# Summing rows on TensorE in loops instead of written-out matmuls

## The chip, the core and the metric

The kernel runs on one core of one Trainium2 chip. The metric is the device time of one execution in microseconds: 718.03 us before the change, the median of three runs (717.57 to 719.21).

## The reference

The input `x` has 384 x 384 pixels of 384 channels in bf16, `w1d` one number. The mean over all pixels gives a value per channel, a sigmoid makes a scale `s` of it, and every pixel is multiplied by that scale:

```python
g = jnp.einsum("bhwc->bc", x) / (H * W)
...
for i in range(k):                      # k is 1
    s = s + gp[:, i:i + C] * w1d[i]
s = _sigmoid(s)
return x * s[:, None, None, :]
```

So all of `x` has to be read before the first output can be written.

## The kernel before

The 147,456 pixels are laid out as 1152 rows. A row is 128 partitions x 384 channels, 96 KB. The whole input is 1152 rows; the buffer `arena` holds 275 of them. The kernel has two stages.

**Reading stage.** SP's queue loads all rows, one DMA for a stretch of rows, into places in `arena` (`load`, L235). TensorE sums them: for each row one matmul of an all-ones matrix (already loaded as weights) with the row's 128 x 384 values, all added up in one PSUM bank (`sum_rows`, L257, the matmul itself in `add_held`, L243, shown as L246 in the profile). 784 rows are *streamed*: summed and overwritten, to be loaded again later (`stream`, L354, "S" in `PLAN`). 368 rows are *kept*. 296 of these are packed: `take` (L364, "K") loads a group and has it summed, `fold` ("F") then packs four rows into the place of three, with bit operations on VectorE (L280 for one input, L286 for joins of two) and a test on ScalarE (L317). 72 rows stay raw; they are loaded last (L425), into areas named U, A, V, Y and T, followed by one last streamed row.

**Writing stage.** ScalarE makes the sigmoid (L433). VectorE and GpSimd unpack and scale the rows (L446), SP stores them (L473), and the streamed rows are loaded once more into places that come free. A planner in the kernel writes this order out; it does not depend on how the sums were made.

What sets the order: each engine runs its instructions in the order in which the kernel adds them to a recorder called `Flow` (L21 to L140). An entry names the rows that it reads and writes; `Flow.emit` turns that into semaphore waits. A DMA that loads into rows waits for the last matmul that summed what stood there, and for the last fold that used them. SP's queue is strictly in order, so a load that waits holds all loads behind it. A first join of a fold overwrites rows, so it waits until TensorE has summed these rows. With one entry a row (L263 to L269) every such wait is for the row concerned. An entry marked `block` has its wait issued by itself, ahead of whatever the entry issues.

`PLAN` (L398) is the order written by hand. An "S" entry has a place in `arena`, a number of rows and, in three entries, a third number: so many rows are summed at once, the rest (`due_rows`) only behind the next kept group, or ahead of the next stream. `keep_warm` (L271) adds 16 matmuls with an all-zero row (`s_bf`) in three places, so that TensorE is not idle for long.

Of the kernel before, what the change touches and what calls it, by code (L numbers as in the profile page):

```python
# [20 lines left out]
class Flow:  # L21
# [47 lines left out]
    def emit(self):  # L69
        nc = self.nc  # L70
        engines = {"SP": nc.sync, "ACT": nc.scalar, "PE": nc.tensor, "DVE": nc.vector, "POOL": nc.gpsimd}

        know = {e: {} for e in engines}

        def covers(k, d):
            return k.get(d.lane, 0) >= d.rank if d.dma else k.get(d.eng, -1) >= d.i

        for s in self.steps:
            k = know[s.eng]
            for d in sorted(s.deps, key=lambda d: -d.i):  # L80
                if covers(k, d):
                    continue
                s.waits.append(d)
                d.wanted = True
                for key, v in d.know.items():
                    if k.get(key, -1) < v:
                        k[key] = v
            s.know = dict(k)
            if s.dma:
                s.know[s.lane] = s.rank  # L90
            else:
                s.know[s.eng] = s.i

        count, sems = {}, {}
        for s in self.steps:
            if not s.dma and s.wanted:
                s.rank = count[s.eng] = count.get(s.eng, 0) + 1

        def sem(s):
            key = s.lane if s.dma else s.eng  # L100
            if key not in sems:
                name = f"f_{key[0]}{key[1]}" if s.dma else f"f_{key}"
                sems[key] = self.tc.alloc_semaphore(name)
            return sems[key]

        last = {}
        with self.tc.tile_critical(sync_engine=mybir.EngineType.Pool, no_gpsimd_drain=True):  # L107
            for s in self.steps:
                eng = engines[s.eng]
                waits = [(sem(d), d.rank * (16 if d.dma else 1)) for d in s.waits]  # L110
                hold = None if s.dma or not waits else waits.pop()
                for h, v in waits:
                    eng.wait_ge(h, v)  # L113
                if s.block and hold:
                    eng.wait_ge(*hold)
                    hold = None
                ins = s.emit()
                if ins is None:
                    continue
                if hold:  # L120
                    ins = ins._wait_ge(*hold)
                if s.dma:
                    ins.then_inc(sem(s), 16)
                    last[s.lane] = s
                elif s.wanted:
                    ins.then_inc(sem(s), 1)
            for lane, s in sorted(last.items(), key=lambda at: at[1].i):
                engines[lane[0]].wait_ge(sem(s), 16 * s.rank)
# [3 lines left out]
def kernel(  # L132
# [11 lines left out]
    nc = tc.nc  # L144
# [5 lines left out]
    RPP = HW // P  # L150
# [10 lines left out]
    U = 3 * PIECE + PAIRS * 3 * PAIR  # L161
    G0 = U + PAIR
    V = G0 + PAIRS * 3 * PAIR
    A = V + PAIR
    N_A = 39
    T = A + N_A
    Y = T + 2 * PIECE
# [19 lines left out]
    ones = pool.tile([P, P], bf16, name="ones")  # L187
# [4 lines left out]
    arena = pool.tile([P, ROWS, C], bf16, name="arena")  # L192
    s_bf = pool.tile([P, C], bf16, name="s_bf")
# [3 lines left out]
    bank0 = psum.tile([P, nc.PSUM_BANK_SIZE_BYTES // 4], f32, name="bank0")  # L197
# [11 lines left out]
    def rows(lo, n):  # L209
        return [("a", r) for r in range(lo, lo + n)]  # L210

    fl = Flow(nc, tc)
# [18 lines left out]


    summed = [0]

    def load(chunk, a, lo, hi):  # L235

        r0, n = chunk
        fl.add(
            "SP",
            lambda: nc.sync.dma_start(out=arena[:, a : a + hi - lo, :], in_=view(xf, r0, n)[:, lo:hi, :]),  # L240
            writes=rows(a, hi - lo), dma=True,
        )
    def add_held(rhs, stop=False):  # L243

        pe = nc.tensor
        return pe.add_instruction(  # L246
            mybir.InstMatmult(
                name=nc.get_next_instruction_name(),
                ins=[pe.lower_ap(rhs), pe.lower_ap(ones[:])],
                outs=[pe.lower_ap(acc)],  # L250
                start_tensor_calc=False, stop_tensor_calc=stop,
                tile_size=(P, P), tile_position=(0, 0), ldweights=False,
            )
        )


    def sum_rows(a, n):  # L257
        def emit(i, first, last):
            if first:
                return nc.tensor.matmul(acc, lhsT=ones[:], rhs=arena[:, i, :], start=first, stop=last)  # L260
            return add_held(arena[:, i, :], last)

        for i in range(a, a + n):  # L263
            first, last = summed[0] == 0, summed[0] == RPP - 1
            fl.add(
                "PE", lambda i=i, f=first, l=last: emit(i, f, l),
                reads=[("a", i), "ones"], writes=["bank0"],
            )
            summed[0] += 1  # L269

    def keep_warm(n):  # L271


        for _ in range(n):
            fl.add("PE", lambda: add_held(s_bf[:]), reads=["s_bf", "ones"], writes=["bank0"])

    def bits(dst, src, op0, s0, op1, s1, reads, writes):
        fl.add(
# [17 lines left out]
    def fold(k):  # L296
# [46 lines left out]
        reads=["ones", "w_bf"], writes=["bank0"],  # L343
# [4 lines left out]
        reads=["bank0"], writes=["w_sc"],  # L348
# [2 lines left out]
    streamed = [0]  # L351
    N_WARM = 16

    def stream(a, n, at_once=None):  # L354

        load(STREAMED, a, streamed[0], streamed[0] + n)
        if n > 40 and streamed[0] > N_STREAM // 2:
            keep_warm(N_WARM)
        m = n if at_once is None else at_once
        sum_rows(a, m)  # L360
        streamed[0] += n
        return a + m, n - m

    def take(g, lo=0, hi=None):  # L364

        a, q = GROUPS[g]
        hi = 4 * q if hi is None else hi
        load(KEPT, a + lo, c_group[g] + lo, c_group[g] + hi)
        sum_rows(a + lo, hi - lo)

    def of_group(g):
        return [i for i, piece in enumerate(pieces) if piece[0] == g]
# [20 lines left out]
    for i, (lo, hi, corner) in enumerate(corners):  # L393
# [2 lines left out]
    take(FIRST)  # L396
    fold(0)
    PLAN = [  # L398
# [6 lines left out]
    ]  # L405
    due_rows = (A, 0)
    for kind, a, *more in PLAN:
        if kind == "S":
            sum_rows(*due_rows)
            due_rows = stream(a, *more)  # L410
        elif kind == "K":
            take(a, *more)
            sum_rows(*due_rows)
            due_rows = (A, 0)
        else:
            for k in of_group(a):
                if not more or k == of_group(a)[more[0]]:
                    fold(k)
    assert streamed[0] == N_STREAM

    def take_raw(a, n):
        load(KEPT, a, raw(a), raw(a) + n)
        sum_rows(a, n)

    for a, n in [(U, 8), (A, 20), (A + 20, 11), (A + 31, 8), (V, 8), (Y + 1, 6), (T + 5, 4), (T + 2, 3), (T, 2)]:  # L425
        take_raw(a, n)
    load(STREAMED, LAST_ROW, N_STREAM, N_STREAM + 1)
    sum_rows(LAST_ROW, 1)
# [5 lines left out]
        reads=["bank0", "w_sc"], writes=["s_bf"],  # L434
# [291 lines left out]
    while True:  # L726
# [12 lines left out]
        if dve_at <= now:  # L739
# [4 lines left out]
            if landed and (ahead < PENDING or not can):  # L744
                chunk, a, lo, n, end = landed.popleft()
# [7 lines left out]
                if end or ahead < MERGE:  # L753
                    b, first = since
                    send(chunk, b, first, lo + n, stored(b, lo + n - first))
                    since = None
            elif can:
                f, t, then = turns.popleft()
# [5 lines left out]
        if alongside and alongside[0][0] <= now:  # L764
            _, chunk, a, lo, n = alongside.popleft()
            store(chunk, a, lo, lo + n)
            moves.append([now + LAT, n * ROW + PER_STORE, stored(a, n)])
        while waiting and waiting[0][0] <= now:
            _, n, then, chunk, a, lo, known = waiting.popleft()
# [14 lines left out]
        if bank_at is None and len(line) <= total - BANKS_AT and got and max(got)[0] > PS * 4 // 3:  # L784
            a = max(got)[1]
# [11 lines left out]
        if got and todo < N_STREAM:  # L797
            n, a = max(got)
            n = min(n, CAP, N_STREAM - todo)
# [62 lines left out]
```

## Time and profile before

| | before |
|---|---|
| median of 3 runs | 718.03 us (717.57 to 719.21) |
| span of the profiled execution | 715.5 us; no other time of this execution is given |
| moved by DMA | 303.68 MB, mean 424 GB/s |
| TensorE busy | 211.7 us, 1202 matmuls |
| VectorE busy | 467.4 us |
| ScalarE busy | 116.5 us |
| GpSimd busy | 98.1 us |
| TensorE waited for loads, in all | 46.9 us, 14 times |
| VectorE's joins waited for TensorE | 10.7 us, 6 times |

The page cuts the span into 40 slices of 17.9 us. The digits of an engine are tenths of busy time, those of PEclk tenths of full TensorE clock, and DMA is the mean busy share of the 16 DMA engines. In a timeline, a row has the start and the length of a run of equal instructions in us, the engine, the line and operation, the tiles, the shape and the count; the brackets have the idle time just ahead and what ended it. The chain of work lists what ended last, followed back from release to release. In a table of windows the columns are the window, its length, busy us and count of PE, PEld, DVE, ACT and POOL, then the granted TensorE clock, the DMA share and GB/s. A row of DMA issues ends with the size and the time from issue to landing.

### The profile page before, as it was taken

The page shows a single profiled execution, that of the slowest core. Times are in us where ns is not written, and L with a number is a line of the kernel's source. Part 1 is how long each engine was busy: PE and PEld are TensorE (multiplying, and loading weights), DVE is VectorE, ACT ScalarE, POOL GpSimd, SP SyncE. Part 2 cuts the span into 40 slices and gives each one's busy share as a digit, 9 for nine tenths or more (in the row PEclk, how much of TensorE's full clock was granted, in tenths as well). Part 3 has the DMA queues.
Part 4 walks back from the last instruction along what each step waited for, and adds up shares of the span by engine and source line. Part 5 has one row for each costly group of instructions (what it writes and reads, how often), then busy time and mean ns, then how long its engine had stood idle before and what let it go on. Part 6 is the DMA issues. An engine that isn't in the chain of part 4 may idle for free.

```text
span 715.5 us, 2029 instructions
## 1 busy us (share of the span) xinstructions
PE 211.7 (30%) x1202; PEld 0.3 (0%) x3; DVE 467.4 (65%) x383; ACT 116.5 (16%) x97; POOL 98.1 (14%) x46
## 2 busy tenths in 40 slices
PE   5667967999598680000000000000000000000000
PEld 0000000000000000000000000000000000000000
DVE  4600001799989849999999999999940597007840
ACT  3700001476667630000110000000000000000000
POOL 0000000000000005414233431167100000000000
PEclk9899998999899995555555555555555555555555
DMA  9999999999999989999999999999999999999997
GB/s 382 428 447 419 439 431 428 452 416 433 426 431 426 429 351 379 405 412 433 430 431 437 438 422 440 434 438 437 440 418 453 420 444 439 419 439 440 439 417 338
DMA packets 15996, 303.68 MB, mean 424 GB/s; under 512 B 1778, under 2 KB 2418, under 8 KB 5106
## 3 DMA queue, kind: packets, MB, share of 16 engines
q1 hardware_dynamic: 15984, 303.57, 99.1%
q8 instruction: 4, 0.07, 0.0%
q14 instruction: 6, 0.05, 0.0%
q10 hardware_dynamic: 2, 0.00, 0.0%
HBM read 190.32 MB, written 113.25 MB: 424 GB/s over the span
## 4 chain that ended last, share of the span: by engine, by line
DMA 48%; DVE 29%; PE 16%; ACT 1%; issue 1%; DVEq 0%; SPq 0%; another core or an unknown queue 0%; POOLq 0%
DMA arena<-in_x_dram 37%; DVE arena L446 20%; PE bank L246 16%; DMA out_dram<-arena 12%; DVE arena L280 5%; DVE arena L286 4%; ACT arena L317 1%; DVEq L107 0%; SPq L473 0%; SPq L240 0%; ACT s_bf L433 0%; SPq L113 0%; SPq L857 0%; POOLq L107 0%
## 5 line engine op out<-in xcount | busy, mean ns | idle before, releaser
L246 PE MATMUL bank<-arena,ones 128*128 128x384 bf16 x1151 | 203.6, 341 | 47.0 <-DMA arena<-in_x_dram 46.9
L280 DVE TENSOR_SCALAR arena<-arena 128x1536 uint16<-128x1536 uint16 (+2 forms) x199 | 140.4, 750 | 105.7 <-DMA arena<-in_x_dram 98.8
L446 POOL TENSOR_TENSOR arena<-arena,s_bf 128x768 bf16<-128x768 bf16 (+3 forms) x42 | 97.9, 2336 | 426.3 <-ACT bank L437 268.0
L446 DVE TENSOR_TENSOR arena<-arena,bank 128x3072 bf16<-128x3072 bf16 (+13 forms) x61 | 138.0, 2304 | 4.3 <-DMA arena<-in_x_dram 3.6
L446 DVE TENSOR_TENSOR arena<-arena,s_bf 128x5376 bf16<-128x5376 bf16 (+4 forms) x27 | 76.5, 2901 | 95.1 <-DMA arena<-in_x_dram 84.9
L286 DVE TENSOR_TENSOR arena<-arena 128x3072 uint16<-128x3072 uint16 (+2 forms) x90 | 117.6, 1307 | 13.5 <-PE bank L246 10.7
L317 ACT ACTIVATE arena<-arena 128x3072 uint16<-128x3072 uint16 (+1 forms) x38 | 102.4, 2696 | 146.0 <-DVE arena L280 146.0
L563 PE MATMUL bank<-odd,ones 128*128 128x1 bf16 x1 | 0.2, 185 | 259.4 <-DVE odd L558 259.4
L384 ACT COPY arena<-bank 128x512 uint32<-128x512 uint32 (+2 forms) x8 | 4.2, 533 | 87.3 <-DMA out_dram<-arena 87.2
L246 PE MATMUL bank<-s_bf,ones 128*128 128x384 bf16 x48 | 8.3, 326 | 0.0
L317 ACT ACTIVATION_READ_ACCUMULATOR arena<-arena 128x1 f32 x38 | 7.1, 186 | 0.0
L384 ACT COPY bank<-arena 128x512 uint32<-128x512 uint32 (+2 forms) x8 | 3.8, 528 | 0.0
L260 PE MATMUL bank<-arena,ones 128*128 128x384 bf16 x1 | 0.5, 477 | 6.8 <-DMA arena<-in_x_dram 6.8
L433 ACT ACTIVATE s_bf<-bank,w_sc 128x384 bf16<-128x384 f32 x1 | 0.6, 581 | 9.5 <-PE bank L246 9.5
L830 ACT ACT_TABLE_LOAD x1 | 1.3, 1283 | 0.7 <-PEq L846 0.7
L337 DVE MEMSET ones<- 128x128 bf16 x1 | 0.2, 165 | 1.1 <-PEq L846 1.1
L342 PE MATMUL bank<-w_bf,ones 1*128 1x1 bf16 x1 | 0.2, 182 | 2.1 <-DMA w_bf<-in_w1d_dram 2.1
L347 DVE TENSOR_SCALAR w_sc<-bank 128x1 f32<-128x1 f32 x1 | 0.2, 158 | 0.9 <-PE bank L342 0.9
L567 DVE CAST odd_i<-bank 128x1 int32<-128x1 f32 x1 | 0.2, 159 | 0.3 <-PE bank L563 0.3
L437 ACT COPY bank<-s_bf 128x192 uint32<-128x192 uint32 x1 | 0.3, 322 | 0.0
L563 PEld LDWEIGHTS bank<-odd,ones 128*128 128x128 bf16 x1 | 0.1, 103 | 517.7 <-DVE odd L558 517.7
L384 ACT COPY arena<-rest 128x64 uint32<-128x64 uint32 x1 | 0.2, 244 | 0.0
(10 smaller groups left out, 1.4 us busy)
## 6 DMA issues: line engine op xcount, KB each, us to landing
arena<-in_x_dram SPq DMA_DIRECT2D x3, 6912.0 KB, 36.2
out_dram<-arena SPq DMA_DIRECT2D x3, 6912.0 KB, 28.4
arena<-in_x_dram SPq DMA_DIRECT2D x4, 4608.0 KB, 24.5
arena<-in_x_dram SPq DMA_DIRECT2D x6, 3072.0 KB, 19.6
out_dram<-arena SPq DMA_DIRECT2D x6, 3072.0 KB, 21.6
arena<-in_x_dram SPq DMA_DIRECT2D x2, 6144.0 KB, 31.5
arena<-in_x_dram SPq DMA_DIRECT2D x2, 4992.0 KB, 23.1
arena<-in_x_dram SPq DMA_DIRECT2D x1, 8160.0 KB, 26.5
```

Of the source, the lines that this page charges most:

```text
L246: return pe.add_instruction(mybir.InstMatmult(name=nc.get_next_instruction_name(), ins=[pe.lower_ap(rhs), pe.lower_ap(ones[:])], outs=[pe. ...
L260: return nc.tensor.matmul(acc, lhsT=ones[:], rhs=arena[:, i, :], start=first, stop=last)
L280: lambda: nc.vector.tensor_scalar(out=dst, in0=src, scalar1=s0, scalar2=s1, op0=op0, op1=op1),
L286: "DVE", lambda: nc.vector.tensor_tensor(out=dst, in0=a, in1=b, op=op), reads=reads, writes=writes
L317: lambda: nc.scalar.activation(out=y, in_=y, func=ACTF.Copy, accum_out=seen[:, 2 * k + i : 2 * k + i + 1]),
L337: fl.add("DVE", lambda: nc.vector.memset(ones[:], 1.0), writes=["ones"])
L384: "ACT", lambda: nc.scalar.copy(dst.bitcast(u32), src.bitcast(u32)), reads=reads, writes=writes
L433: lambda: nc.scalar.activation(out=s_bf[:], in_=acc, func=ACTF.Sigmoid, scale=w_sc[:, 0:1]),
L437: "ACT", lambda: nc.scalar.copy(s_ps.bitcast(u32), s_bf[:].bitcast(u32)), reads=["s_bf"], writes=["bank0"]
L446: lambda: vec.tensor_tensor(out=v, in0=v, in1=s[:, None, :].to_broadcast([P, n, C]), op=Op.mult),
L563: lambda: nc.tensor.matmul(votes, lhsT=ones[:], rhs=odd[:], start=True, stop=True),
L830: nc.scalar.preload_act_table(ACTF.Sigmoid)
```

## The change

Three things change, all in the reading stage.

- **Loops.** `sum_rows` adds a stretch of 16 rows or more as one `block` entry that holds a hardware loop on TensorE, and the one to three rows left over as single matmuls. The number of matmuls a turn is picked from 4, 5 and 3 by the number of instructions that it leaves; here it is 3 for all 27 loops, which take 966 rows in 322 turns. The loop entry and the rows behind it read the whole stretch, so whoever waits for one row of it waits for the last matmul of the stretch. `keep_warm` becomes a loop of 4 matmuls a turn.
- **Nothing put off.** The third numbers in `PLAN` are gone: every stream is summed whole before the group behind it.
- **Sizes.** The stream of 80 rows has 84, the last one 15 in place of 19 and starts four rows higher; the loads of A are 24 and 7 rows in place of 20 and 11.

```diff
+    BODY, LOOPED = 4, 16
...
-        for i in range(a, a + n):
-            first, last = summed[0] == 0, summed[0] == RPP - 1
+        def looped(a, m, body):
+            with nc.Fori(a, a + m, body, engines=[mybir.EngineType.PE]) as i:
+                for j in range(body):
+                    add_held(arena[:, bass.ds(i + j, 1), :])
+            return None
+
+        if summed[0] == 0:
+            fl.add("PE", lambda i=a: emit(i, True, False), reads=[("a", a), "ones"], writes=["bank0"])
+            summed[0] += 1
+            a, n = a + 1, n - 1
+        m = 0
+        if n >= LOOPED:
+            body = min((4, 5, 3), key=lambda b: 2 * b + (n - 1) % b)
+            m = (n - 1) // body * body
+        if m:
             fl.add(
-                "PE", lambda i=i, f=first, l=last: emit(i, f, l),
-                reads=[("a", i), "ones"], writes=["bank0"],
+                "PE", lambda a=a, m=m, b=body: looped(a, m, b), reads=rows(a, m) + ["ones"], writes=["bank0"], block=True
+            )
+            summed[0] += m
+        for i in range(a + m, a + n):
+            last = summed[0] == RPP - 1
+            fl.add(
+                "PE", lambda i=i, l=last: emit(i, False, l),
+                reads=rows(a, n) if m else [("a", i), "ones"], writes=["bank0"],
             )
             summed[0] += 1
...
-        for _ in range(n):
-            fl.add("PE", lambda: add_held(s_bf[:]), reads=["s_bf", "ones"], writes=["bank0"])
+        def looped():
+            with nc.Fori(0, n, BODY, engines=[mybir.EngineType.PE]):
+                for _ in range(BODY):
+                    add_held(s_bf[:])
+            return None
+
+        fl.add("PE", looped, reads=["s_bf", "ones"], writes=["bank0"], block=True)
...
-        ("S", 156, 80), ("K", 1), ("F", 1), ("S", 68, 48), ("K", 2), ("F", 2), ("S", 172, 52), ("K", 3), ("F", 3),
-        ("S", 68, 48), ("K", 4), ("S", 220, 39, 16), ("K", 5), ("F", 4), ("F", 5), ("S", 92, 24, 19), ("S", 196, 24),
+        ("S", 156, 84), ("K", 1), ("F", 1), ("S", 68, 48), ("K", 2), ("F", 2), ("S", 172, 52), ("K", 3), ("F", 3),
+        ("S", 68, 48), ("K", 4), ("S", 220, 39), ("K", 5), ("F", 4), ("F", 5), ("S", 92, 24), ("S", 196, 24),
...
-    for a, n in [(U, 8), (A, 20), (A + 20, 11), (A + 31, 8), (V, 8), (Y + 1, 6), (T + 5, 4), (T + 2, 3), (T, 2)]:
+    for a, n in [(U, 8), (A, 24), (A + 24, 7), (A + 31, 8), (V, 8), (Y + 1, 6), (T + 5, 4), (T + 2, 3), (T, 2)]:
```

The order of TensorE's instructions at the end of the reading stage, before the change: the last stream of 19 rows (it waits for f_SP8, the semaphore of its load), the 8 rows of U (f_SP9), the first 20 rows of A (f_SP10) and its next 11 (f_SP11).

```order
L246 MATMUL bank_71<-arena,ones 128x384 [waits f_SP8]
L246 MATMUL bank_71<-arena,ones 128x384 x18
L246 MATMUL bank_71<-arena,ones 128x384 [waits f_SP9]
L246 MATMUL bank_71<-arena,ones 128x384 x7
L246 MATMUL bank_71<-arena,ones 128x384 [waits f_SP10]
L246 MATMUL bank_71<-arena,ones 128x384 x19
L246 MATMUL bank_71<-arena,ones 128x384 [waits f_SP11]
```

The same place after the change. The stream has 15 rows. The load into A has 24: the wait for it stands at the jump into a loop, whose body is three register programs (shown as ISA) and three matmuls with an add and a branch, run seven times; three matmuls follow.

```order
L247 MATMUL bank_71<-arena,ones 128x384 [waits f_SP8]
L247 MATMUL bank_71<-arena,ones 128x384 x14
L247 MATMUL bank_71<-arena,ones 128x384 [waits f_SP9]
L247 MATMUL bank_71<-arena,ones 128x384 x7
L265 UNCONDITIONAL_BRANCH [waits f_SP10]
L265 ISA
L247 MATMUL bank_71<-arena,ones 128x384
L247 ISA
L247 MATMUL bank_71<-arena,ones 128x384
L247 ISA
L247 MATMUL bank_71<-arena,ones 128x384
L265 REGISTER_ALU
```

What moved: four rows from ahead of that load to behind its wait, and the wait from a matmul to the loop's entry.

VectorE in one fold of a kept group of 32 rows, before: the three joins that overwrite summed rows wait for f_PE (TensorE) by themselves, one in the first half of the fold, one at its end and one in the next half.

```order
L286 TENSOR_TENSOR arena<-arena 128x3072 [waits f_DVE,f_PE]
L280 TENSOR_SCALAR arena<-arena 128x1536 [waits f_ACT]
L280 TENSOR_SCALAR arena<-arena 128x1536
L280 TENSOR_SCALAR arena<-arena 128x1536 [waits f_DVE]
L280 TENSOR_SCALAR arena<-arena 128x1536
L286 TENSOR_TENSOR arena<-arena 128x1536 [waits f_DVE,f_PE]
L286 TENSOR_TENSOR arena<-arena 128x1536 [waits f_DVE]
L280 TENSOR_SCALAR arena<-arena 128x3072 [waits f_ACT]
```

After: only the first join of the group waits for TensorE, and that wait is for the last matmul of the group.

```order
L310 TENSOR_TENSOR arena<-arena 128x3072 [waits f_DVE,f_PE]
L304 TENSOR_SCALAR arena<-arena 128x1536 [waits f_ACT]
L304 TENSOR_SCALAR arena<-arena 128x1536
L304 TENSOR_SCALAR arena<-arena 128x1536 [waits f_DVE]
L304 TENSOR_SCALAR arena<-arena 128x1536
L310 TENSOR_TENSOR arena<-arena 128x1536 [waits f_DVE] x2
L304 TENSOR_SCALAR arena<-arena 128x3072 [waits f_ACT]
```

What moved: the later joins' waits for TensorE are gone, and the first one has to wait for 32 rows.

More of the change, by code (lines that the diff above doesn't have):

```diff
@@ L352, with stream @@
     N_WARM = 16
-    def stream(a, n, at_once=None):
+    def stream(a, n):
         load(STREAMED, a, streamed[0], streamed[0] + n)
@@ L358, in stream @@
             keep_warm(N_WARM)
-        m = n if at_once is None else at_once
-        sum_rows(a, m)
+        sum_rows(a, n)
         streamed[0] += n
-        return a + m, n - m
     def take(g, lo=0, hi=None):
@@ L398 @@
     PLAN = [
[3 rows of a table removed]
[3 rows of a table added]
         ("K", 6), ("F", 6), ("S", 220, 20), ("K", 7, 24, 32), ("S", 240, 19), ("K", 7, 0, 12), ("F", 7, 0),
         ("S", 220, 20), ("K", 7, 12, 24), ("S", 240, 19), ("K", 8, 0, 12), ("S", 220, 20), ("K", 8, 24, 32),
[1 row of a table removed]
[1 row of a table added]
     ]
-    due_rows = (A, 0)
     for kind, a, *more in PLAN:
         if kind == "S":
-            sum_rows(*due_rows)
-            due_rows = stream(a, *more)
+            stream(a, *more)
         elif kind == "K":
             take(a, *more)
-            sum_rows(*due_rows)
-            due_rows = (A, 0)
         else:
```

4 rows, old and new, of the table PLAN are left out of this document.

## The prediction

> **What bounds the kernel now.** I read the page first, then the chain of work that ended last, then TensorE's timeline. In the page I look at the span, at what the engines did, and at the two strips "PE" and "DMA".
>
> ```profile
> span 715.5 us, 2029 instructions
> PE 211.7 (30%) x1202; PEld 0.3 (0%) x3; DVE 467.4 (65%) x383; ACT 116.5 (16%) x97; POOL 98.1 (14%) x46
> PE   5667967999598680000000000000000000000000
> DMA  9999999999999989999999999999999999999997
> HBM read 190.32 MB, written 113.25 MB: 424 GB/s over the span
> ```
>
> The DMA engines are busy from end to end; moving bytes is the bound. TensorE works only in the first 15 of 40 slices. The change moves no byte, so it can matter at one place: where the reading stage ends and everything waits for the sums. The chain there reads (start, length, what):
>
> ```profile
> 245.00 11.81 DMA arena<-in_x_dram
> 256.85 10.59 PE bank L246 x63
> 267.46 0.59 ACT s_bf L433
> 268.07 12.70 DVE arena L446 x11
> ```
>
> The last large load lands at 256.8, TensorE adds 63 rows without a break until 267.4, then come the sigmoid, the first scaling and the first store. All that follows starts from there, so a microsecond at 267.4 is a microsecond at the end. No time is given for the profiled execution apart from its span; 718.03, the median of the runs, lies 2.5 us above the span, and I add shifts to 718.03.
>
> TensorE's timeline gives its pace, and what stood ahead of each burst (idle us, then what ended it):
>
> ```profile
> 38.50 11.79 PE L246 MATMUL bank<-arena,ones 128*128 128x384 bf16 x62 [3.71 <-DMA arena<-in_x_dram]
> 53.45 10.89 PE L246 MATMUL bank<-arena,ones 128*128 128x384 bf16 x66 [3.16 <-DMA arena<-in_x_dram]
> 68.31 19.39 PE L246 MATMUL bank<-arena,ones 128*128 128x384 bf16 x108 [3.97 <-DMA arena<-in_x_dram]
> ...
> 167.36 13.16 PE L246 MATMUL bank<-arena,ones 128*128 128x384 bf16 x80 [0.33 <-DMA arena<-in_x_dram]
> 183.44 2.76 PE L246 MATMUL bank<-arena,ones 128*128 128x384 bf16 x16 [2.93 <-DMA arena<-in_x_dram]
> 190.71 34.19 PE L246 MATMUL bank<-arena,ones 128*128 128x384 bf16 x194 [4.50 <-DMA arena<-in_x_dram]
> 227.28 5.36 PE L246 MATMUL bank<-arena,ones 128*128 128x384 bf16 x32 [2.39 <-DMA arena<-in_x_dram]
> 234.28 5.20 PE L246 MATMUL bank<-arena,ones 128*128 128x384 bf16 x31 [1.64 <-DMA arena<-in_x_dram]
> 241.56 6.68 PE L246 MATMUL bank<-arena,ones 128*128 128x384 bf16 x40 [2.08 <-DMA arena<-in_x_dram]
> 250.44 4.55 PE L246 MATMUL bank<-arena,ones 128*128 128x384 bf16 x27 [2.20 <-DMA arena<-in_x_dram]
> 256.85 10.57 PE L246 MATMUL bank<-arena,ones 128*128 128x384 bf16 x63 [1.86 <-DMA arena<-in_x_dram]
> ```
>
> 80 matmuls in 13.16 us is 164.5 ns each, the pace at full clock. After 3.71 us of idling 62 took 11.79, not 10.20; after 3.97, 108 took 19.39, not 17.77: 1.6 us lost each time. After 3.16 nothing was lost (66 in 10.89). The 63 at the end come after 1.86 us and run at full pace.
>
> **The change part by part.**
>
> *Last loads (+0.9).* The first load into A grows from 20 to 24 rows. The rows behind it are 63 in both: 20+11+8+8+6+4+3+2+1 and 24+7+8+8+6+4+3+2+1. The stretch
>
> ```profile
> 112.00:172.00 60.00, 59.67 (x353) 0.00 (x0) 42.63 (x59) 32.29 (x23) 0.00 (x0) 0.96 1.00 431
> ```
>
> moves 431 GB/s, so a row (128 x 384 x 2 bytes = 98,304 B) takes 0.228 us, and four make the load land 0.9 us later, with as much work behind it. The four rows taken from the last stream went to the 84-row one, so the loads before stand where they stood.
>
> *Clock at the tail (+1.6).* TensorE now has 15+8 rows, not 19+8, ahead of that load: it finishes 4 x 0.168 = 0.7 us sooner (4.55/27 each) and waits 0.9 longer. Idle: 1.86+0.7+0.9 = 3.4 us, and 3.7 with the loop's entry (next). That is the 3.71 of the burst at 38.50, which lost 1.6 us. Bounds: 0 (the 3.16 row) and 1.6; I take 1.6, the nearest row. The granted clock (the third number from the end) shows how sharp this is:
>
> ```profile
> 184.00:188.40 4.40, 2.21 (x14) 0.00 (x0) 4.17 (x7) 3.31 (x3) 0.00 (x0) 1.00 1.02 441
> 188.50:191.80 3.30, 1.09 (x4) 0.00 (x0) 2.79 (x4) 1.93 (x3) 0.00 (x0) 0.50 1.04 447
> ```
>
> The burst at 183.44 ended at 186.2, and the clock had halved by 188.5, after 2.3 us of idling. [...]
>
> *Loops: pace (0) and entry (+0.3).* By the code 966 rows go through 27 loops, all with three matmuls a turn, 322 turns. A turn has 3 x 164.5 = 493 ns of matmul to hide three register programs, one add and one branch. The trace shows no register instruction on TensorE; the nearest rows are its own branch and semaphore step, beside SP's branch (min/median/max ns):
>
> ```profile
> L857 PEldq EVENT_SEMAPHORE  x2: 51/51/51, 714.8 to 715.5; - x2
> L857 SPq COMPARE_BRANCH  x1: 33/33/33, 0.7 to 0.7; - x1
> ...
> L857 PEldq COMPARE_BRANCH  x1: 168/168/168, 0.8 to 0.8; - x1
> ```
>
> With 51 for each register step, 4 x 51 + 168 = 372 ns, hidden, with 121 ns left to issue three matmuls. If each costs 168, 5 x 168 = 840 ns, 280 a row. I take hidden, being nearer the plain step; the other end is rival 2. Below zero is excluded: the matmuls themselves are unchanged. At an entry the wait stands ahead of a register move and a jump, so the first matmul follows a landing by 51+168 and a register program: 0.3 us. It counts once on the path, after the 24-row load; earlier entries fall into idle time or behind queued matmuls.
>
> *Kept rows: later folds (0).* A loop reads its load as one block, so VectorE's first join of a group waits for all 32 rows, where it waited for 8. VectorE's timeline:
>
> ```profile
> 128.71 1.76 DVE L286 TENSOR_TENSOR arena<-arena 128x3072 uint16<-128x3072 uint16 x1 [7.43 <-PE bank L246]
> ...
> 208.95 1.90 DVE L280 TENSOR_SCALAR arena<-arena 128x3072 uint16<-128x3072 uint16 x3 [2.17 <-DMA arena<-in_x_dram]
> 211.18 1.76 DVE L286 TENSOR_TENSOR arena<-arena 128x3072 uint16<-128x3072 uint16 x1 [0.33 <-PE bank L246]
> 240.37 0.96 DVE L280 TENSOR_SCALAR arena<-arena 128x3072 uint16<-128x3072 uint16 x1 [0.20 <-ACT arena L317]
> 243.37 1.03 DVE L280 TENSOR_SCALAR arena<-arena 128x1536 uint16<-128x1536 uint16 x2 [2.04 <-DMA arena<-in_x_dram]
> ```
>
> For the join at 128.71 TensorE had to do 80+8 matmuls; now 84+32: 28 x 0.1645 = 4.6, plus 0.9 for the larger load, 5.5 us. For the join at 211.18 it is 24 x 0.1645 = 3.9. After that only 0.20+2.04 us of VectorE's waiting can absorb it, so the last fold ends some 1.7 us later (up to 5.5 if little is absorbed). Behind it SP holds the load into V and all smaller ones. Those have cover (KB, us from issue to landing; V's, the kept group's at 97.7, and the very first, which met an empty queue):
>
> ```profile
> arena<-in_x_dram SPq DMA_DIRECT2D x1, 768.0 KB, 7.1
> ```
> ```profile
> arena<-in_x_dram SPq DMA_DIRECT2D x1, 3072.0 KB, 21.6
> ```
> ```profile
> arena<-in_x_dram SPq DMA_DIRECT2D x1, 2400.0 KB, 8.1
> ```
>
> An empty queue costs 8.1 - 25 x 0.228 = 2.4 us. V's 8 rows move in 1.8, so 7.1-1.8-2.4 = 2.9 us of delay is free: 1.7 costs nothing, 5.5 would land the last row 2.6 us later, near 269.5, still before TensorE ends. The load of the first kept group now waits for 64 rows of the stream that it overwrites, not 16: 48 x 0.1645 = 7.9 us, against 21.6-7.3-2.4 = 11.9 free.
>
> *Sums no longer put off (0).* The order changes only at group 5: 23 rows of the 39-row stream come ahead of its 32. They take 3.8 us and fall into the 4.50 us that TensorE idled before 190.71. SP's 27 extra jumps at 33 ns each come while it waits for loads to come free.
>
> Sum: 0.9 + 1.6 + 0.3 = +2.8: the sums end near 270.2, the kernel at 718.03 + 2.8 = **720.8**. As the loads end before that, TensorE alone sets it.
>
> **Rivals.** *1, the clock stays up:* +1.2, 719.2. For it: 3.4 us lies between 3.16 (kept) and 3.71 (lost). Against: the halving after 2.3 us.
>
> *2, the loop cannot be issued in 493 ns.* At 600 ns a turn, the 197 turns after 111.8 cost 21 us more, against 17.9 us that TensorE idles there (0.33+2.93+4.50+2.39+1.64+2.08+2.20+1.86): 722 to 739 as none or all of it shows, say 730. At 840 ns it is 68 us, or 768 to 786. It decides once a turn passes 493 ns. For it: TensorE's 168 ns branch is five times SP's. [...] The trace has TensorE's fetches as packets, four in the reading stage, one here between 50 and 60 us (packets, MB, share of 16 engines):
>
> ```profile
> q8 instruction: 1, 0.02, 0.6%
> ```
>
> [...]
>
> *3, faster: those packets stood in the loads' way.* If all four hit the same DMA engine, they delay its last load by 3.8 us; a program with 281 matmuls for 1202 needs about one, so loads land 2.9 us sooner. With the clock up: 718.03 - 2.9 + 1.2 = 716.3; with the 1.6 lost, 717.9, no change. It decides if the packets add up on one engine. Against: four in 213 us, and TensorE's own 10.6 us behind the load stays.
>
> **How the numbers follow.** 720.8: 0.35. Rival 1: 0.15. Rival 2: 0.22 around 730, 0.05 at 768 and more; 2b 0.05. Rival 3: 0.10 at 716.3, 0.08 at 717.9. A measurement can tell about 0.2%, 1.4 us, from no change. Slower: 0.35+0.22+0.05+0.05 = 0.67; same (719.2, 717.9): 0.15+0.08 = 0.23; faster: 0.10. The range 717.0 to 733.0 leaves out rival 3's fast end and the upper part of rival 2, about 0.2; 720.8 alone would have 719 to 722.
>
> **What would show it.** Right: TensorE's last burst of 63 begins near 258, after over 3 us of idling, with a granted clock of 0.50 at its start, and ends near 270. Rival 2: bursts of loops over 170 ns a row, VectorE's joins late by tens of us. Rival 3: fewer instruction packets and the last loads landing before 266. I am wrong if the sums end at 267.5 or sooner.

## The result and the profile after

The changed kernel takes 739.38 us (median of four runs, 739.23 to 740.54); the kernel before, run beside it on the same chip, 718.15 us (717.57 to 719.21). The ratio is 1.0291, 95% interval 1.0272 to 1.031: 21.2 us slower. The forecast was 720.8, its range ended at 733.0. The profiled execution of after took 740.54 us, with a span of 738.2; its span is 22.7 us longer than that of before.

The page of after, the lines that answer to those of before, and the strip of DMA rates:

```profile
span 738.2 us, 3668 instructions
PE 243.7 (33%) x1202; PEld 0.3 (0%) x3; DVE 467.2 (63%) x383; ACT 116.5 (16%) x97; POOL 98.1 (13%) x46
PE   4689988999899877000000000000000000000000
DMA  9999999989597996999999999999999999999997
GB/s 392 434 431 431 454 400 423 441 341 409 231 419 325 414 424 238 404 421 421 430 436 443 428 438 425 433 445 421 438 441 435 434 422 439 432 426 441 443 431 316
```

The number of matmuls is the same (1202), but they keep TensorE busy for 243.7 us instead of 211.7, and 16 slices instead of 15 have TensorE in them. The DMA strip, all 9s in the reading stage before but for an 8 at its end, now has 8, 5, 7 and 6 in it, with 231 to 341 GB/s in the four worst slices: loads came late. From slice 17 on the DMA engines are as busy as before.

The end of the reading stage in the chain of waits of after:

```profile
265.34 10.92 DMA arena<-in_x_dram
276.26 0.23 issue
276.49 13.32 PE bank L247 x63
289.81 0.02 issue
289.83 0.59 ACT s_bf L451
290.42 0.02 issue
290.45 12.70 DVE arena L464 x11
```

The pieces are the same as before, but the sums end at 289.81, not at 267.44: 22.4 us of the 22.7. The last burst itself grew only from 10.59 to 13.32; the other 20 us are that it starts at 276.49 and not at 256.85. So the cause lies ahead of the tail. TensorE's timeline of after:

```profile
53.88 54.69 PE L247 MATMUL bank<-arena,ones 128*128 x238 [0.33 <-DMA arena<-in_x_dram]
111.91 26.87 PE L247 MATMUL bank<-arena,ones 128*128 x116 [3.34 <-DMA arena<-in_x_dram]
138.62 2.76 PE L247 MATMUL bank<-s_bf,ones 128*128 128x384 bf16 x16
...
183.92 0.65 PE L247 MATMUL bank<-arena,ones 128*128 x3 [0.27 <-issue]
184.84 0.65 PE L247 MATMUL bank<-arena,ones 128*128 x3 [0.27 <-issue]
...
200.76 44.65 PE L247 MATMUL bank<-arena,ones 128*128 x215 [0.16 <-issue]
246.32 6.54 PE L247 MATMUL bank<-arena,ones 128*128 x32 [0.91 <-DMA arena<-in_x_dram]
253.45 6.37 PE L247 MATMUL bank<-arena,ones 128*128 x31 [0.59 <-DMA arena<-in_x_dram]
260.73 7.84 PE L247 MATMUL bank<-arena,ones 128*128 x40 [0.90 <-DMA arena<-in_x_dram]
269.03 3.90 PE L247 MATMUL bank<-arena,ones 128*128 128x384 bf16 x23 [0.47 <-DMA arena<-in_x_dram]
276.49 13.31 PE L247 MATMUL bank<-arena,ones 128*128 x63 [3.56 <-DMA arena<-in_x_dram]
```

Before, TensorE worked in bursts and idled for a load ahead of nearly each. Now 238 rows run in one piece, at 54.69/238 = 230 ns a row where full clock gives 164.5, and between 111.91 and 245 it waits for no load at all. It is no longer ahead of the loads; it paces them. The chain of waits from 111.9 to 289.8, by line, says the same: TensorE makes up 77.6% of it, and loads are on it only from 239.10 on (before, from 111.8 to 267.4, TensorE has 60.3% and loads 32.2%):

```profile
by line: PE bank L247 77.6%; DMA arena<-in_x_dram 15.4%; issue 7.1%
```

What fills the time are the loops' own instructions on TensorE's sequencer (the part of the engine that issues its instructions, PEldq in the rows), all at the loop's line (duration min/median/max in ns, then first and last start), and the register programs in front of the other matmuls of a turn:

```profile
L265 PEldq FUSED_REGOPS  x322: 59/59/59, 9.4 to 280.7; - x161
L265 PEldq ALU_OP  x322: 36/36/42, 9.8 to 281.1; - x161
L265 PEldq COMPARE_BRANCH  x322: 76/208/341, 9.9 to 281.2; - x161
```
```profile
L247 PEldq FUSED_REGOPS  x644: 55/55/55, 9.6 to 280.9; - x161
```

322 turns, as counted. The five steps of a turn take 59 + 2 x 55 + 36 + 208 = 413 ns. The turn takes longer than they do. One loop seen alone (the adds between 95 and 107 us):

```profile
L265 PEldq ALU_OP  x17: 36/36/36, 95.0 to 106.5; - x17
```

Sixteen turns in 11.5 us are 0.72 us a turn, 240 ns a row. The loads bring a row every 228 ns.

VectorE and SP show what hangs on that. The joins that overwrite summed rows waited 39.9 us for TensorE, seven times, where it was 10.7 us and six times before (the last figure of the row):

```profile
L310 DVE TENSOR_TENSOR arena<-arena 128x3072 uint16<-128x3072 uint16 (+2 forms) x90 | 117.7, 1307 | 42.1 <-PE bank L247 39.9
```

SP issues its last nine loads, from the 24 rows for A on, between 265.34 and 282.3 (the row has the start of the first and the time to the end of the last); before, the last one goes out at 260.2:

```profile
265.34 16.98 SPq L241 DMA_DIRECT2D arena<-in_x_dram  x9
```

### The profile page after: what moved, and what is told of

Read it like the earlier page. It is cut to its first block, busy times and chain, and to the rows that moved or that the text cites. A ratio compares the mean times of both kernels' runs of the same rounds, so it can differ in the third digit from the quotient of the medians.

```text
span 738.2 us, 3668 instructions
## 1 busy us (share of the span) xinstructions
PE 243.7 (33%) x1202; PEld 0.3 (0%) x3; DVE 467.2 (63%) x383; ACT 116.5 (16%) x97; POOL 98.1 (13%) x46
## 4 chain that ended last, share of the span: by engine, by line
DMA 40%; DVE 28%; PE 24%; issue 3%; SPq 0%; DVEq 0%; another core or an unknown queue 0%; ACT 0%; POOLq 0%
DMA arena<-in_x_dram 29%; PE bank L247 24%; DVE arena L464 20%; DMA out_dram<-arena 11%; DVE arena L304 5%; DVE arena L310 3%; DVEq L107 0%; SPq L491 0%; SPq L241 0%; ACT s_bf L451 0%; SPq L113 0%; SPq L875 0%; POOLq L107 0%; DVEq L113 0%
## 5 line engine op out<-in xcount | busy, mean ns | idle before, releaser
L247 PE MATMUL bank<-arena,ones 128*128 (+1 forms) x1151 | 235.7, 333 | 37.1 <-DMA arena<-in_x_dram 18.4
L310 DVE TENSOR_TENSOR arena<-arena 128x3072 uint16<-128x3072 uint16 (+2 forms) x90 | 117.7, 1307 | 42.1 <-PE bank L247 39.9
L261 PE MATMUL bank<-arena,ones 128*128 128x384 bf16 x1 | 0.5, 479 | 7.0 <-DMA arena<-in_x_dram 7.0
```

The costliest lines, as they stand in the source:

```text
L247: return pe.add_instruction(mybir.InstMatmult(name=nc.get_next_instruction_name(), ins=[pe.lower_ap(rhs), pe.lower_ap(ones[:])], outs=[pe. ...
L310: "DVE", lambda: nc.vector.tensor_tensor(out=dst, in0=a, in1=b, op=op), reads=reads, writes=writes
```

## The experiments

**Theory A**, formed from the trace of after: the issue of a turn sets the pace of TensorE, 240 ns a row; as that is over the 228 ns of the loads, TensorE falls behind them, loads that overwrite its rows are issued late, and the delay reaches the end. (In the first expectations below, the point where a turn begins to cost is still the matmuls' own time, 164.5 ns a row; the 228 came later.) Beside that the two terms of the tail (larger load, clock) stand as predicted. **Theory B**: it is not the pace but the waits. A loop is one block that reads a whole stretch, so folds and loads behind it wait for its last row; with plain matmuls and the same waits it would be as slow. All ratios are against runs of before on the same chip.

**A longer body** (e1_body8): eight matmuls a turn in place of three, all else as after.

```diff
-            body = min((4, 5, 3), key=lambda b: 2 * b + (n - 1) % b)
+            body = 8
```

> Eight matmuls a turn in place of three, all else as in the changed kernel. Theory A (a turn costs TensorE's sequencer about 365 ns for add and branch and 114 ns for each row, 707 ns for three rows, and that pace holds up loads and folds): 365 + 8 x 114 = 1277 ns is under 8 x 164.5 = 1316 ns, so the loop hides and the time falls from 739 to 718 to 722 us. Theory B (the waits for a whole stretch, not the pace, hold up folds and loads): the stretches are the same, so it stays at 735 us or above.

Measured: 721.32 us, ratio 1.0037 (1.0025 to 1.005). 18 of the 21 us are gone with the waits and the sizes left as they were. Theory B falls for the bulk.

**No loops** (e2_no_loops): the code of after with a threshold that no stretch reaches, so that the rows' matmuls are written out and waits are by row; new sizes, nothing put off. The zero matmuls of `keep_warm` stay a loop, here and in e4_block_waits.

```diff
-    BODY, LOOPED = 4, 16
+    BODY, LOOPED = 4, 10 ** 6
```

> The changed kernel with every row again a matmul of its own and a wait of its own; nothing is put off and the sizes are the new ones. Theory A and theory B both: most of the 21 us is gone. By the tail term of the prediction (24-row load 0.9 us later, clock halved after 3.4 us of idling 1.6 us): 719 to 720.7 us. If that term was wrong: 718.0 to 718.5 us.

Measured: 720.6 us, 1.0016 (1.0005 to 1.0028). Its stretch from the same burst (112.7) to the end of the sums, beside that of after, in windows of each:

```profile
112.70:272.00 159.30, 140.75 (x807) 0.00 (x0) 118.87 (x160) 91.41 (x64) 0.00 (x0) 0.95 0.97 412
```
```profile
111.90:289.80 177.90, 159.35 (x807) 0.00 (x0) 118.63 (x160) 91.41 (x64) 0.00 (x0) 0.97 0.89 370
```

The same 807 matmuls take 18.6 us longer, at a mean clock that is no lower (0.97 against 0.95), and the DMA rate falls from 412 to 370 GB/s. Without loops TensorE is idle for 159.30 - 140.75 = 18.55 us, waiting for loads. In after 18.55 us are left free too, but only 0.91+0.59+0.90+0.47+3.56 = 6.4 of them are waits for loads (timeline above); the rest are gaps in and between turns. So the loops stretch the work by 30.7 us: 12.1 of them fill what had been waits for loads, 18.6 come out at the end.

**The wide waits alone** (e4_block_waits): the loop entry stays one block with the wait for the whole stretch, but its matmuls are written out.

```diff
-            with nc.Fori(a, a + m, body, engines=[mybir.EngineType.PE]) as i:
-                for j in range(body):
-                    add_held(arena[:, bass.ds(i + j, 1), :])
+            for i in range(a, a + m):
+                add_held(arena[:, i, :])
```

> The changed kernel with the loops written out as matmuls in a row, but with the waits for a whole stretch kept. Theory A: 718 to 721 us. Theory B: 735 us or above. What it has over the kernel without loops and with waits by row is the price of the wide waits alone; the prediction put it at 0.

Measured: 722.64 us (5 runs), 1.0046 (1.0031 to 1.006), 2.0 us above the one without loops and 1.6 above the range that theory A gave. The first join of a fold that has to wait, in e4_block_waits and in e2_no_loops (VectorE's timelines; the idle time ahead is in the brackets):

```profile
134.35 1.76 DVE L309 TENSOR_TENSOR arena<-arena 128x3072 uint16<-128x3072 uint16 x1 [12.26 <-PE bank L247]
...
217.45 1.76 DVE L309 TENSOR_TENSOR arena<-arena 128x3072 uint16<-128x3072 uint16 x1 [3.30 <-PE bank L247]
```
```profile
129.73 1.76 DVE L310 TENSOR_TENSOR arena<-arena 128x3072 uint16<-128x3072 uint16 x1 [7.52 <-PE bank L247]
...
212.59 1.76 DVE L310 TENSOR_TENSOR arena<-arena 128x3072 uint16<-128x3072 uint16 x1 [0.81 <-PE bank L247]
```

4.6 and 4.9 us later: the wait for 32 rows in place of 8 is there. SP's last eight loads, behind the large one for A, in before, e2_no_loops and e4_block_waits:

```profile
252.42 7.76 SPq L240 DMA_DIRECT2D arena<-in_x_dram  x8
```
```profile
253.98 9.69 SPq L241 DMA_DIRECT2D arena<-in_x_dram  x8
```
```profile
253.00 11.86 SPq L241 DMA_DIRECT2D arena<-in_x_dram  x8
```

The last load goes out at 260.2, 263.7 and 264.9. So 3.5 us of its delay are there without the wide waits, which add 1.2. Between 260 and 262 the DMA rate of e4_block_waits falls to 203 GB/s (364 in e2_no_loops):

```profile
260.00:262.00 2.00, 2.00 (x7) 0.00 (x0) 1.97 (x3) 2.00 (x1) 0.00 (x0) 0.50 0.72 203
```

Theory B holds as a small term. Its size is not sure: with these waits and harmless loops 721.32 was measured (e1_body8), so 0.7 to 2.0 us, and only the upper of the two is clear of noise. Nor do the two profiled executions show it as a later end, since both end their sums near 272.0, and that of e2_no_loops, at 722.42, was its slowest run. By what path the wide waits reach the end is thus not shown.

**The loops alone** (e3_loops_alone): the loops of after (three a turn) with the plan of before: its sizes, and its sums put off. As an edit of after:

```diff
-        ("S", 156, 84), ("K", 1), ("F", 1), ("S", 68, 48), ("K", 2), ("F", 2), ("S", 172, 52), ("K", 3), ("F", 3),
-        ("S", 68, 48), ("K", 4), ("S", 220, 39), ("K", 5), ("F", 4), ("F", 5), ("S", 92, 24), ("S", 196, 24),
+        ("S", 156, 80), ("K", 1), ("F", 1), ("S", 68, 48), ("K", 2), ("F", 2), ("S", 172, 52), ("K", 3), ("F", 3),
+        ("S", 68, 48), ("K", 4), ("S", 220, 39, 16), ("K", 5), ("F", 4), ("F", 5), ("S", 92, 24, 19), ("S", 196, 24),
...
-    for a, n in [(U, 8), (A, 24), (A + 24, 7), (A + 31, 8), (V, 8), (Y + 1, 6), (T + 5, 4), (T + 2, 3), (T, 2)]:
+    for a, n in [(U, 8), (A, 20), (A + 20, 11), (A + 31, 8), (V, 8), (Y + 1, 6), (T + 5, 4), (T + 2, 3), (T, 2)]:
```

> Loops of three as in the changed kernel, but with the plan of before: sums put off as before, last stream of 19 rows, loads of A of 20 and 11. Theory A: the loops carry the loss, 736 to 743 us. If the sizes and the missing delay carry a good part of it: under 730 us.

Measured: 737.37 us, 1.0253 (1.0237 to 1.0269). The loops alone, with their wide waits, are 19.0 (737.37 - 718.38) of the 21 us.

**Where the turn begins to cost** (e5_body5, e8_body4): five and four matmuls a turn. The edit is the one line of e1_body8 with 5 and 4.

> Five matmuls a turn, all else as in the changed kernel. Theory A: 365 + 5 x 114 = 935 ns a turn, 187 ns a row, 22 ns over the matmul's own 164.5; three a turn were 71 ns over. The loss that goes with the pace shrinks to about a third: 722 to 726 us, turns of 935 ns in the trace. If a loop cost by its number of turns and not by pace, 3/5 of it would stay: 730 us or more.

> Four a turn. Theory A: 365 + 4 x 114 = 821 ns, 205 ns a row, 41 ns over: between the kernels with three and with five, 727 to 732 us.

Measured: with five 721.68 us, 1.004 (1.0028 to 1.0053); with four 724.27 us, 1.0088 (1.0068 to 1.0109). The turns are as long as expected, but both times lie below the expected ranges, the second by nearly 3 us: the expectations had every turn over its matmuls' 164.5 ns a row cost something. The adds of one loop with five and of one with four:

```profile
L265 PEldq ALU_OP  x13: 36/36/36, 114.3 to 125.7; - x13
```
```profile
L265 PEldq ALU_OP  x13: 36/36/36, 116.3 to 126.3; - x13
```

Twelve turns in 11.4 and 10.0 us: 0.95 us a turn of five, 0.83 of four, so 0.12 us for each matmul more and a fixed 0.36 to 0.38. Per row that is 190 and 208 ns; three give 240.

| a turn | us a turn | ns a row | matmul in it, us | time, us |
|---|---|---|---|---|
| written out, same waits | | 164.5 | | 722.64 |
| 8 | matmul sets it | 164.5 | 1.32 | 721.32 |
| 5 | 0.95 | 190 | 0.82 | 721.68 |
| 4 | 0.83 | 208 | 0.66 | 724.27 |
| 3 | 0.72 | 240 | 0.49 | 739.38 |

Turns of five and four are longer than their matmuls too, and yet five cost nothing that can be told and four 1.6 to 3 us. (Five and four were run on another chip, where before took 718.67 us and not 718.38.) With four TensorE still gets free of work and waits for loads, as its timeline shows where after has no wait between 111.91 and 245:

```profile
203.67 4.78 PE L247 MATMUL bank<-arena,ones 128*128 x24 [0.35 <-DMA arena<-in_x_dram]
210.93 16.50 PE L247 MATMUL bank<-arena,ones 128*128 x91 [2.47 <-DMA arena<-in_x_dram]
```

The price jumps between 208 and 240 ns a row, on the two sides of the loads' 228; no run lies between them. Theory A stands, with the loads' pace in place of the matmuls' as the point where a turn begins to cost.

**Threes early only** (e10_threes_early) and **streams in eights** (e9_streams_in_eights): before's plan, sizes and waits by row for kept groups; loops of three in the first streams only, or loops of eight in all streams. The loop code and the looped `keep_warm` of after come with both.

```diff
-    def sum_rows(a, n):
+    def sum_rows(a, n, loops=False):
...
+        if loops and n >= LOOPED:
...
-        sum_rows(a, m)
+        sum_rows(a, m, streamed[0] < 300)
```

With eights, `body = 8` stands in place of the choice and the call is `sum_rows(a, m, True)`.

> As the run with eights, but loops of three, and only in the first six streams (until about 105 us), where TensorE waits for loads. A turn of 707 ns is 235 ns a row, hardly over the 228 ns in which a row is loaded. Theory A with the pace of the loads as its point of decision: TensorE falls behind by a few us and catches up later, within 1.5 us of before. If every slow turn counted: 113 turns of 707 ns in place of 493 would add 24 us.

> The plan and sizes of before, loops of eight for the streamed rows alone; kept groups written out with a wait for each row. If what is left of the kernel with eight a turn (2.7 us over before) is the wide wait at the kept groups and the new sizes, this is within 1 us of before. If a loop costs something by itself, it stays 2 us or more over. If fewer instruction fetches help, it falls under before.

Measured: 718.28 us, 0.9999 (0.9989 to 1.001), and 718.49 us, 1.0 (0.9989 to 1.001). Only five streams got loops of three, with 92 turns and not 113: of the sixth, six rows are summed at once, too few for a loop, and the rest by a call without loops. By the sum of the expectation 92 turns would still add 20 us. Loops of three for these 276 rows cost nothing where written-out matmuls follow and let TensorE catch up (its burst of 40 rows begins at 241.55, in before at 241.56). And the eights bring nothing either, though the program has fewer matmul instructions: nothing beats before.

**The sizes alone** (e6_sizes_alone) and **nothing put off alone** (e7_nothing_put_off), each put into before.

```diff
-        ("S", 156, 80), ("K", 1), ("F", 1), ("S", 68, 48), ("K", 2), ("F", 2), ("S", 172, 52), ("K", 3), ("F", 3),
+        ("S", 156, 84), ("K", 1), ("F", 1), ("S", 68, 48), ("K", 2), ("F", 2), ("S", 172, 52), ("K", 3), ("F", 3),
...
-        ("F", 7, 1), ("F", 8, 0), ("K", 8, 12, 24), ("S", 240, 19), ("F", 8, 1),
+        ("F", 7, 1), ("F", 8, 0), ("K", 8, 12, 24), ("S", 244, 15), ("F", 8, 1),
...
-    for a, n in [(U, 8), (A, 20), (A + 20, 11), (A + 31, 8), (V, 8), (Y + 1, 6), (T + 5, 4), (T + 2, 3), (T, 2)]:
+    for a, n in [(U, 8), (A, 24), (A + 24, 7), (A + 31, 8), (V, 8), (Y + 1, 6), (T + 5, 4), (T + 2, 3), (T, 2)]:
```
```diff
-        ("S", 156, 52), ("S", 92, 62), ("S", 26, 66), ("S", 160, 60), ("S", 108, 48), ("S", 28, 64, 6),
+        ("S", 156, 52), ("S", 92, 62), ("S", 26, 66), ("S", 160, 60), ("S", 108, 48), ("S", 28, 64),
...
-        ("S", 68, 48), ("K", 4), ("S", 220, 39, 16), ("K", 5), ("F", 4), ("F", 5), ("S", 92, 24, 19), ("S", 196, 24),
+        ("S", 68, 48), ("K", 4), ("S", 220, 39), ("K", 5), ("F", 4), ("F", 5), ("S", 92, 24), ("S", 196, 24),
```

> The kernel before with the three sizes alone (84 rows, last stream of 15, loads of A of 24 and 7). By the tail term of the prediction, TensorE idles about 3.4 us ahead of its last 63 rows, these take 12 us and not 10.4, and the kernel takes 719 to 720.7 us. If the term was wrong: the idle time stays under 2.5 us or the burst at 10.4 us, and the time within 0.5 us of before.

> The kernel before with every stream summed whole, nothing put off. The prediction costs it at nothing, as 3.8 us of matmuls fall into 4.5 us of idling: within 0.7 us of before. Rival: the fold of group 5 starts later and the time goes up by 1 us or more.

Measured: the sizes 720.39 us, 1.0017 (1.0006 to 1.0028); nothing put off 718.85 us, 0.9999 (0.9989 to 1.0009). The last burst with the new sizes, and the clock in it (third number from the end):

```profile
257.84 12.08 PE L246 MATMUL bank<-arena,ones 128*128 128x384 bf16 x63 [3.43 <-DMA arena<-in_x_dram]
```
```profile
255.43:258.84 3.41, 1.00 (x7) 0.00 (x0) 3.34 (x6) 2.79 (x2) 0.00 (x0) 1.00 0.94 393
258.84:262.25 3.41, 3.41 (x12) 0.00 (x0) 0.00 (x0) 0.06 (x1) 0.00 (x0) 0.50 0.99 408
```

It starts 1.0 us later than before (256.85), after 3.43 us of idling. One us into it the clock halves, for 3.41 us, and the burst takes 12.08 us in place of 10.57.

**The sizes with TensorE kept busy** (e11_sizes_kept_warm, e12_sizes_warm16): the sizes alone, and behind the 8 rows of U 8 or 16 matmuls of the zero row.

```diff
         take_raw(a, n)
+        if a == U:
+            keep_warm(8)
```

(16 in the second)

> The kernel before with the three sizes, and 8 more matmuls with an all-zero row behind the rows of U, ahead of the 24-row load of A. Tail term: idle 3.4 - 1.3 = 2.1 us, the clock stays up, the last 63 rows take 10.4 us, and only the 0.9 us of the later load is left: 718.7 to 719.6 us. If the clock has no part in it: as with the sizes alone, 720.4 us.

> The sizes alone with 16 zero matmuls behind the 8 rows of U, so that TensorE ends some 2.6 us later and idles for about 0.8 us ahead of the last burst. If the clock carries the tail's loss beside the larger load (theory A): the 63 matmuls take about 10.4 us in the profiled execution, and the time is 718.7 to 719.5. If the larger load alone carries it, or the loss has nothing to do with idling: 720.2 to 720.6, as the sizes alone.

Measured: with 8 720.25 us, 1.0021 (1.0012 to 1.0031), a miss; with 16 719.38 us, 1.0012 (1.0003 to 1.0021). TensorE's last burst, first with 8, then with 16:

```profile
257.98 12.08 PE L246 MATMUL bank<-arena,ones 128*128 128x384 bf16 x63 [2.17 <-DMA arena<-in_x_dram]
```
```profile
258.68 10.40 PE L246 MATMUL bank<-arena,ones 128*128 128x384 bf16 x63 [0.86 <-DMA arena<-in_x_dram]
```

Eight left 2.17 us idle, and that was still enough for the clock to halve (0.50 from 259 to 260 us), which the expectation had not reckoned with. With sixteen 0.86 us are left and the 63 matmuls run at full clock (1.00 from 258 to 268 us), 1.68 us shorter. That the idling makes the burst slow is shown by these traces. How much of the median it carries is not: the intervals of the three kernels with the new sizes overlap, and the runs of each fall apart by 1.5 to 2.4 us (e6_sizes_alone from 718.55 to 720.94). That 719.38 lies in the expected range shows nothing either, since before took 717.91 on that chip: over before, the three kernels are 1.7, 1.6 and 1.5 us longer. In the profiled execution of e12_sizes_warm16 the burst also began 0.8 us later than with the sizes alone (258.68 and 257.84), which took half of the gain back.

## Why the prediction was wrong

**Loops: pace (0): the step that failed.** The prediction put five steps at 4 x 51 + 168 = 372 ns, below the 493 ns of three matmuls, and called them hidden. The steps' own times were near: 413 ns. What was missing is the time from one to the next and the issue of three matmuls that are addressed by registers: the turn takes 0.72 us, 0.31 more than the steps (0.06 for each of the five), while the prediction had left 0.12 for all of it. Its upper bound, 0.84 us, lay on the right side of the truth; taking the low end because one of two known rows was short decided the forecast. The term, put at 0, measures 17 to 18 us (739.38 against the 721.3 to 722.6 of the kernels whose loops or matmuls keep up with the loads).

**Rival 2** was the mechanism, with two errors. Its point of decision, 493 ns a turn, is wrong: turns of four and five pass their matmul time and cost 3 us or less. What counts is a row's time against the loads' 228 ns, 0.68 us for a turn of three. And its price: by its own sum 0.72 us a turn would give 197 x (0.72-0.493) = 44.7 us, less the 17.9 of idling, 744.8; measured is 739.38. The stretch grew by 30.7, of which 12.1 were absorbed. Some 8 of the 14 us between 30.7 and 44.7 are that e2_no_loops does not run all at full clock (its 140.75 us of matmuls would be 807 x 0.1645 = 132.75); the rest was not settled row by row. The range ended at 733 because it left out the upper part of this rival; with 0.27 on it, the 739 had to be inside.

**Rival 2b** (0.05 of the chances), that loops bring more instruction packets, fell; no run shows such a term. After, with 27 loops, has two in the whole run, before has four:

```profile
q8 instruction: 2, 0.03, 0.0%
```

One loop is slower than the others, 0.92 us a turn (the rows at 183.92 and 184.84 above): 15 turns, about 3 us. In e8_body4 two turns begin 1.02 us apart, at 247.21 and 248.23, in place of 0.83. In after no packet moves between 180 and 195 us, where that loop runs; one does soon behind it, between 195 and 198. The cause was not tested and stays open.

**Rival 3** (its 3.8 us: four packets of 0.96 us, as one took 0.6% of 16 engines' time in 10 us) fell: after has two packets in place of four and is slower, e5_body5 with two is no faster than e1_body8 with three, and e9_streams_in_eights and e10_threes_early, with three, are no faster than before.

**Last loads (+0.9)** was right: 1.0 in the profiled execution of e6_sizes_alone. **Clock at the tail (+1.6)** was right in size in the traces: idle 3.43 (predicted 3.4), 1.5 us lost, and in after 3.56 and a burst of 13.31. Its ground was not: it took the length of the idling, between the 3.16 that kept the clock and the 3.71 that lost it, to decide, and 2.17 us lost it in e11_sizes_kept_warm. So that it came true in these executions was in part luck (last section). The median with the sizes alone is 1.7 above that of before, less than the 2.5 of the two terms. That some executions keep the clock, which is rival 1, would explain it, but only one execution of each kernel was profiled, so it is not shown.

**Loops' entry (+0.3)**: 0.23 us in the chain of after from the landing to the first matmul, against 0.04 before.

**Kept rows: later folds (0)** was mis-sized. The first join was late by what was said (5.5 us predicted, 5.6 against before in e4_block_waits, at 134.35), the second by more (3.9 and 6.3, at 217.45; 1.4 of that is there in e2_no_loops too). But the prediction let VectorE's gaps and the 2.9 us of V's load absorb it; the wide waits cost 0.7 to 2.0 us in place of 0. The last load went out 4.7 us later than before, 1.2 of it by these waits; whether that is the path is not shown.

**Sums no longer put off (0)** was right (0.9999), and so was that the change acts by the end of the reading stage alone. What would show it wrong, bursts of loops over 170 ns a row and joins late by tens of us, is what the trace showed.

## What to carry to other kernels

The turn of three took 0.72 us here, 0.31 more than the durations of its own steps (0.413) add up to; measure a turn from start to start, or take the sum of durations as a lower bound only. Compare it with the pace of whatever feeds the engine, not only with the engine's own work: over the loads' 228 ns a row, loops at 240 cost 17 to 18 us here; under it a loop that slowed the engine by a sixth (190 ns a row for 164.5) cost nothing that could be told. An engine with 30% of the span busy can still come to set the end, as TensorE did here with its sums 22.4 us later: its idle time counts only in the stage where it works.

## What the runs showed of the hardware

In the loops of this kernel a turn took 0.72 us with three matmuls (after), 0.83 with four (e8_body4) and 0.95 with five (e5_body5): about 0.36 us, and 0.12 us for each matmul that is addressed by a register. The branch in it is recorded with 0.21 us.

The clock halved after less idling than the 3.71 us of the burst at 38.50: 2.17 us was enough in the profiled execution of e11_sizes_kept_warm, and 2.21 in that of e7_nothing_put_off, where 27 matmuls took 6.20 us:

```profile
250.75 6.20 PE L246 MATMUL bank<-arena,ones 128*128 128x384 bf16 x27 [2.21 <-DMA arena<-in_x_dram]
```

In before, 2.20 us at the same place cost nothing (4.55). The granted clock changes 13 times in the profile of before, between 21.20 and 270.38 us, and 7 times in that of after, between 23.02 and 292.67. From one change to the next it is always a whole multiple of 3.41 us: 1 to 22 of them in before, 1 to 47 in after. The windows below are the pieces of 3.41 us into which a profile's own points of change cut its time. For the two at this place, first in before, then in e7_nothing_put_off, the first figure behind the window is its length, the next TensorE's busy time:

```profile
246.48:249.90 3.42, 1.75 (x11) 0.00 (x0) 3.39 (x6) 2.66 (x1) 0.00 (x0) 1.00 0.96 406
249.90:253.31 3.41, 2.87 (x18) 0.00 (x0) 3.18 (x5) 2.38 (x3) 0.00 (x0) 1.00 1.07 457
```
```profile
247.32:250.74 3.42, 1.22 (x8) 0.00 (x0) 3.26 (x6) 2.86 (x2) 0.00 (x0) 1.00 1.01 428
250.74:254.15 3.41, 3.40 (x11) 0.00 (x0) 3.30 (x4) 2.72 (x2) 0.00 (x0) 0.50 1.03 440
```

In before the idling of 2.20 us is cut by the end of a window, which has 1.67 us of it; in e7_nothing_put_off one window has it all, and the next one runs at half clock. In the profiles of before and after, 11 windows at full clock were followed by half clock, and TensorE was idle for 2.25 us or more in each; in the 132 others at full clock it was idle for 1.90 us at most. With the 0.86 us of e12_sizes_warm16 the clock stayed at 1.00. By these counts an idling of 3.43 us, as with the new sizes, could be split between two windows so that neither has more than 1.90 us of it, and the clock would stay; that is an estimate from before and after, and no run shows it.
